# A PSUM bank for the convolution and tanh of a feed-forward, and another written order for its kernel

## The chip, the cores and the metric

The kernel runs on one core of a Trainium2 chip. The metric is the device time of one execution in microseconds (us). Three runs of the kernel before gave 747.68, 746.42 and 743.80 us, median 746.42. A separate execution was profiled; its own time was 744.24 us, and the span from its first to its last instruction 742.5 us.

Engines are called PE (matrix unit), DVE (vector), ACT (scalar, activations), POOL (GpSimd) and SP (issues the DMAs). Each runs its own instructions strictly in the order in which they were written for it, and waits on semaphores where it needs another engine's result.

## What is computed

```python
# q, k, v: (8, 8, 576, 64); window 128, ALiBi slopes per head
scores = q @ k.T / 8 + bias(slope, rel);  scores[not (0 <= rel < 128)] = -1e9
attn = softmax(scores);  x = (attn @ v) -> (batch, seq, 512)
h = relu(x @ w_in)                      # 512 -> 1024
conv_out[s] = sum_k conv_w[k] * h[s + k - 1]    # 3 taps along the sequence, zeros at its ends
out = (h * sigmoid(conv_out)) @ w_out   # 1024 -> 512
```

`w_in`, `conv_w` and `w_out` come in as 64-bit floats. The chip turns each into two single-precision parts, high and low, and every product with them is three matmuls: high by high, low by high, high by low.

## The kernel before

The 8 x 576 tokens are 36 tiles of 128. For each tile t and each half u of the heads (4 heads): `qkT` transposes q and k through PE, `scores` multiplies them against the keys of tiles t-1 and t, `merge` (DVE, L283 and L296) puts the window together in PSUM and adds the bias, `rowmax` (L300) and `exps` (ACT, L305) and `normal` (DVE, L316 to L318) make the softmax, `attnT` transposes it (L325, copied out by ACT, L328), two POOL masks (L331, L334) cut it into the sides of the window, and `av` multiplies by v. `x_hi` (ACT, L363) and `x_lo` (DVE, L367) split the result; `xfin` (L382, L384) copies one column of it to the neighbouring chunk. Some tiles lie at the joint of two sequences: tiles 4, 5, 13, 14, 22, 23, 31 and 32 need a second mask in each of their four merges, and tiles 0, 9, 18 and 27 begin a sequence and have only one side.

Two tiles make a chunk of 256 tokens for the feed-forward. A chunk has four steps, each for 256 of the 1024 hidden columns. A step is: `up_half` twice (24 matmuls, L406, then ACT's relu L410 to `hh` and the middle tap L411 to `z`), `conv` (DVE, L421: the outer two taps, for each of two halves, so four instructions, more at a joint), `gate` (ACT's tanh L429 in place, DVE L430), `split` (ACT L438, POOL L439) and `down` (12 matmuls, L454, into two PSUM banks that gather over the chunk's four steps). `hh` and `z` lie in SBUF, two buffers each. All other matmul results go through six PSUM banks that are handed out in turn (pool `pst`); `down` has two (`pso`).

A chunk's first step needs the column that `xfin` takes from the tile after the chunk: the matmuls of `up_half` wait for it in every second period.

What sets the order: within `manual_schedule` PE, DVE, ACT and POOL execute what the code calls in the order in which it calls it; SP's order was left to a planner. `opening()` (tiles 0 to 2), three slow periods (tiles 3, 4 and 5, which also convert the weights: `W`, 17 blocks of 128 x 512 or less), then `period(t)` for tiles 6 to 36 with two steps each, then `tail()` with the last four steps. A weight block is clamped by POOL (L130), rescaled by ACT (L131), put together by DVE (L137, L138, L141), rounded to its high part by ACT (L186), and PE (L201, L202) and ACT (L203) make the low part.

Of the kernel before, what the change touches and what calls it, by code (L numbers as in the profile page):

```python
# [8 lines left out]
F32 = mybir.dt.float32  # L9
# [7 lines left out]
P = 128  # L17
# [4 lines left out]
def tile_alibi_window_attention_conv_glu(  # L22
# [28 lines left out]
    pst = ctx.enter_context(tc.tile_pool(name="pst", bufs=6, space=bass.MemoryType.PSUM))  # L51
# [105 lines left out]
    fetched, begun, started = [], [], []  # L157

    def fetch_weight():
        if not blocks:  # L160
            return
        block = blocks.pop(0)
        st = wpool.tile([P, WB, 2], U32, name="wst", tag="wst")
        if block is None:
            n = 3 * NFC
            st = st[:n, :P, :]
            src = moe_conv_w.rearrange("k (f p) -> (k f) p", p=P).bitcast(U32).rearrange("r (p t) -> r p t", t=2)
        else:
# [12 lines left out]

    def convert_weight():
        block, st, g = begun.pop(0)
        f = to_f32(st, g)
        if block is not None:
            nc.scalar.copy(out=block[1][0], in_=f)  # L186
        started.append((block, f))
        fetch_weight()


    def finish_weight():
        block, f = started.pop(0)
        if block is None:
            n = 3 * NFC
            ps = pst.tile([P, n], F32, name="pcw", tag="tr")
            nc.tensor.transpose(ps, f, ident[:n, :n])
            nc.vector.tensor_copy(out=cw.rearrange("p k f -> p (k f)"), in_=ps)
# [14 lines left out]
    raws, vraw, pts, sms, es, rls, avs = {}, {}, {}, {}, {}, {}, {}  # L212
# [45 lines left out]
    def scores(t, u):  # L258
        first, slot, win, prev, cur = window(t)
        e = apool.tile([P, HU, P], F32, name=f"e{t}_{u}", tag="e", bufs=4)  # L260
        st = apool.tile([P, 3, HU], F32, name=f"st{t}_{u}", tag="st", bufs=3)
# [59 lines left out]
    def attnT(t, u):  # L321
# [15 lines left out]
        rls[t, u] = rl  # L337
# [374 lines left out]
```

## Time and profile before

| | us |
|---|---|
| median of three runs | 746.42 |
| time of the profiled execution | 744.24 |
| its span | 742.5 |
| PE busy | 663.2 (89%) |
| DVE busy | 559.9 (75%) |
| ACT busy | 451.7 (61%) |
| POOL busy | 205.0 (28%) |
| longest in the chain that ended last | DVE 52%, ACT 30%, PE 14% |

Busy times are sums over instructions; they say nothing of where an engine stood still. For that one cuts the span into stretches, here three: until the scores of tile 6 begin (150.7 us), until those of tile 35 begin (676.4 us), and the rest. A wait in the profile names the engine whose semaphore came last.

### The profile page before, as it was taken

The numbers are of one execution on the slowest core, as the hardware profiler recorded it, in microseconds if no ns is written. First come the engines' busy times: TensorE is split into PE (matmuls) and PEld (weight loads), VectorE is DVE, ScalarE is ACT, GpSimd is POOL, SyncE is SP. The second block draws the span as 40 slices with busy tenths as digits, with TensorE's granted clock in tenths as the row PEclk, the third lists the DMA queues.
The fourth block names the chain that finished last, engine by engine and source line by source line (L and its number), as shares of the span: only waits on it lengthen the run. The fifth ranks groups of instructions, "written<-read, shape, count | busy, mean of one in ns | idle before, by whom it ended". The sixth has DMA issues, their size and how long they took to land.

```text
span 742.5 us, 13277 instructions
## 1 busy us (share of the span) xinstructions
PE 663.2 (89%) x4881; PEld 565.6 (76%) x4881; DVE 559.9 (75%) x1208; ACT 451.7 (61%) x1274; POOL 205.0 (28%) x234
## 2 busy tenths in 40 slices
PE   6585868699989998999898999899899989998997
PEld 4354546588878887888787888788787878887896
DVE  7767665668887888888887878878888788888552
ACT  4656463566666666666666665666666656566653
POOL 1232222223223223322323333332223223322221
PEclk8878789899999999999999999999999999999999
DMA  9443331121222121212231232222221212100001
GB/s 221 107 128 94 119 87 43 28 73 44 72 57 57 44 72 43 72 44 72 44 86 55 46 86 44 61 55 72 57 59 44 72 43 72 43 29 1 30 1 57
DMA packets 120100, 47.02 MB, mean 63 GB/s; under 512 B 113356, under 2 KB 113380, under 8 KB 120036
## 3 DMA queue, kind: packets, MB, share of 16 engines
q1 hardware_dynamic: 120036, 46.17, 24.6%
q8 instruction: 39, 0.64, 0.4%
q14 instruction: 25, 0.20, 0.1%
HBM read 36.72 MB, written 9.44 MB: 62 GB/s over the span
## 4 chain that ended last, share of the span: by engine, by line
DVE 52%; ACT 30%; PE 14%; issue 3%; POOL 1%; DMA 1%; ACTq 0%; SPq 0%; DVEq 0%; POOLq 0%
DVE z L421 19%; ACT e L305 11%; DVE sc L283 6%; DVE st L300 6%; DVE e L296 6%; PE p L406 5%; ACT z L429 5%; DVE z L430 5%; ACT z L411 4%; PE o L454 4%; DVE x L367 3%; ACT hh L410 2%; ACT x L363 2%; ACT qkT_all L247 2%; DVE e L318 2%
## 5 line engine op out<-in xcount | busy, mean ns | idle before, releaser
L406 PE MATMUL p<-x,wi 128*128 128x258 f32 x1728 | 230.3, 291 | 28.7 <-DVE x L382 28.6
L406 PEld LDWEIGHTS p<-x,wi 128*128 128x128 f32 x1728 | 220.7, 195 | 36.9 <-ACT e L305 31.9
L421 DVE SCALAR_TENSOR_TENSOR z<-hh,cw,z 128x256 f32<-128x256 f32 (+7 forms) x384 | 196.3, 554 | 28.0 <-ACT z L411 24.5
L305 ACT ACTIVATE e<-e,st 128x128 f32<-128x128 f32 x288 | 112.7, 393 | 132.5 <-DVE st L300 132.1
L454 PE MATMUL o<-wo,gh 128*128 128x512 f32 x576 | 187.7, 407 | 2.3 <-ACT wo L203 1.9
L439 POOL TENSOR_TENSOR gl<-z,gh 128x512 fp32r<-128x512 f32 x72 | 94.3, 1309 | 146.7 <-ACT gh L438 142.8
L331 POOL TENSOR_SCALAR_AFFINE_SELECT rl<-rl 128x512 f32<-128x512 f32 x64 | 43.4, 678 | 329.5 <-ACT rl L328 329.2
L454 PEld LDWEIGHTS o<-wo,gh 128*128 128x128 f32 x576 | 103.3, 189 | 28.3 <-issue 4.5
L454 PE MATMUL o<-wo,gl 128*128 128x512 f32 x288 | 114.4, 397 | 0.0
L430 DVE SCALAR_TENSOR_TENSOR z<-z,hh 128x512 f32<-128x512 f32 x72 | 54.7, 760 | 61.5 <-ACT z L429 61.5
L429 ACT ACTIVATE z<-z 128x512 f32<-128x512 f32 x72 | 45.8, 636 | 72.5 <-DVE z L421 72.5
L411 ACT ACTIVATE z<-hh,cw 128x256 f32<-128x256 f32 x144 | 73.5, 510 | 9.2 <-ACT hh L410 0.8
L271 PE MATMUL sc<-qkT_all 64*128 64x256 f32 x512 | 68.8, 409 | 2.6 <-ACT qkT_all L247 2.6
L352 PE MATMUL av<-rl,rv 128*64 128x128 f32 x1088 | 68.7, 278 | 0.7 <-POOL rl L334 0.6
L352 PEld LDWEIGHTS av<-rl,rv 128*64 128x64 f32 x1088 | 59.4, 138 | 12.8 <-issue 7.7
L334 POOL TENSOR_SCALAR_AFFINE_SELECT rl<-rl 128x512 f32<-128x512 f32 x72 | 54.6, 758 | 41.8 <-ACT rl L328 37.4
L271 PEld LDWEIGHTS sc<-qkT_all 64*128 64x128 f32 x512 | 49.3, 197 | 21.0 <-issue 6.1
L296 DVE SCALAR_TENSOR_TENSOR e<-sc,bias 128x256 f32<-128x256 f32 x144 | 61.1, 425 | 4.9
L283 DVE COPY_PREDICATED sc<-m_prev,sc 128x256 f32<-128x256 uint8 x128 | 53.9, 421 | 14.1 <-PE sc L271 14.1
L454 PEld LDWEIGHTS o<-wo,gl 128*128 128x128 f32 x288 | 54.4, 189 | 13.2 <-POOL gl L439 0.2
L410 ACT ACTIVATE hh<-p 128x258 f32<-128x258 f32 x144 | 53.9, 374 | 6.7 <-PE p L406 6.5
L438 ACT CAST gh<-z 128x512 fp32r<-128x512 f32 x72 | 44.5, 618 | 20.1 <-DVE z L430 20.1
(64 smaller groups left out, 651.3 us busy)
## 6 DMA issues: line engine op xcount, KB each, us to landing
out_dram<-ob SPq DMA_DIRECT2D x36, 256.0 KB, 2.2
rqk<-in_q_dram SPq DMA_DIRECT2D x32, 256.0 KB, 3.3
rqk<-in_k_dram SPq DMA_DIRECT2D x32, 256.0 KB, 3.8
rv<-in_v_dram SPq DMA_DIRECT2D x32, 256.0 KB, 3.0
wst<-in_moe_w_in_dram SPq DMA_DIRECT2D x8, 512.0 KB, 4.8
wst<-in_moe_w_out_dram SPq DMA_DIRECT2D x8, 512.0 KB, 3.7
rqk<-in_q_dram SPq DMA_DIRECT2D x8, 128.0 KB, 3.2
rqk<-in_k_dram SPq DMA_DIRECT2D x8, 128.0 KB, 3.2
```

The lines of the kernel that those rows point to most:

```text
L271: nc.tensor.matmul(pss[a][:, g], qt, qkT_all[rows, win, u, 1, g, :], start=True, stop=True)
L283: nc.vector.copy_predicated(out=s_cur, mask=mask.unsqueeze(1).to_broadcast(shp), data=data)
L296: nc.vector.scalar_tensor_tensor(out=heads, in0=s_cur, scalar=-0.125, in1=b, op0=ALU.mult, op1=ALU.add)
L305: nc.scalar.activation(out=e[:, j, :], in_=e[:, j, :], func=AF.Exp, bias=st[:, 0, j : j + 1], scale=-1.0, accum_out=st[:, 1, j : j + 1],)
L352: nc.tensor.matmul(ps[a * D : (a + 1) * D, u * NG + g], vraw[tt][:, u * HU + j], rl[:, side, j], start=n == 0, stop=n == len(sides) - 1,)
L406: nc.tensor.matmul(ps[:, :XW], a[:, cc, f * P : (f + 1) * P], x[:, cc, :], start=n == 0, stop=n == last)
L411: nc.scalar.activation(out=z[:, ff, :], in_=hh[:, ff, 1 : 1 + CW], func=AF.Copy, scale=cw[:, 1, f : f + 1])
L421: nc.vector.scalar_tensor_tensor(out=z[:, ff, a:cut], in0=hh[:, ff, a + kk : cut + kk], scalar=cw[:, kk, f : f + 1], in1=z[:, ff, a:cut], ...
L429: nc.scalar.activation(out=z, in_=z, func=AF.Tanh)
L430: nc.vector.scalar_tensor_tensor(out=z, in0=z, scalar=1.0, in1=hh[:, :, 1 : 1 + CW], op0=ALU.add, op1=ALU.mult)
L439: nc.gpsimd.tensor_tensor(out=gl, in0=z, in1=as32(gh), op=ALU.subtract)
L454: nc.tensor.matmul(oo[m], g[:, ff, ms], w[:, f, :], start=f == 0 and n == 0, stop=f == NFC - 1 and n == 2)
```

## The change

The feed-forward's `z` is now two things. The middle tap, the convolution and the tanh work in place in `zp`, a tile of one PSUM bank with a single buffer (pool `psz`); `gate` reads `zp` and `hh` and writes `z` in SBUF, from which `split` goes on. The bank comes from `pst`, which has five in place of six.

Helpers are cut into smaller pieces (`relu`, `middle`, `conv`, `tanh`, `gate`, `g_hi`, `g_lo`, `down`, `store`; a weight block's six pieces; `attnT` without its copy and masks; `x_lo` without `xfin`), and the order of all of them is written in two strings: OPENING (tiles 0 to 5, steps 0 to 5, all weights) and PERIOD, used from tile 6 on until all is done. In a string, `MA0.1.0` is `merge(t+0, 1, 0)`, `XL-1` is `x_lo(t-1)`, `CV1.0` is `conv(s+1, 0)`, and `V3` is weight block 3's DVE part. SP's order is the written one too. The copy of `cw` out of PSUM moves from DVE to ACT.

```diff
-    pst = ctx.enter_context(tc.tile_pool(name="pst", bufs=6, space=bass.MemoryType.PSUM))
+    pst = ctx.enter_context(tc.tile_pool(name="pst", bufs=5, space=bass.MemoryType.PSUM))
+    psz = ctx.enter_context(tc.tile_pool(name="psz", bufs=1, space=bass.MemoryType.PSUM))
...
-            nc.scalar.activation(out=z[:, ff, :], in_=hh[:, ff, 1 : 1 + CW], func=AF.Copy, scale=cw[:, 1, f : f + 1])
+    def middle(s, ff):
+        f = 2 * (s % NFP) + ff
+        if s not in zps:
+            zps[s] = psz.tile([P, 2, CW], F32, name=f"zp{s}", tag="zp")
+        nc.scalar.activation(
+            out=zps[s][:, ff, :], in_=hhs[s][:, ff, 1 : 1 + CW], func=AF.Copy, scale=cw[:, 1, f : f + 1]
+        )
...
+    def conv(s, ff):
+        c, f = s // NFP, 2 * (s % NFP) + ff
+        hh, z = hhs[s], zps[s]
...
+    def tanh(s):
+        nc.scalar.activation(out=zps[s], in_=zps[s], func=AF.Tanh)
+
+    def gate(s):
+        zgs[s] = fpool.tile([P, 2, CW], F32, name=f"z{s}", tag="z", bufs=2)
+        nc.vector.scalar_tensor_tensor(
+            out=zgs[s], in0=zps.pop(s), scalar=1.0, in1=hhs.pop(s)[:, :, 1 : 1 + CW], op0=ALU.add, op1=ALU.mult
+        )
...
+    OPENING = """
+    Q0 QO0 CL0 S0.0 Q1 MA0.0.0 RS0 MA0.0.1 V0 S0.1 MA0.1.0 RM0.0 MA0.1.1 QO1 CL1 Q2 H0 P0 CL2 QO2 RS1 V1
...
+    PERIOD = """
+    S0.0 S0.1 MA0.0.0 AV-1 MA0.0.1 D-2 OB-2 XH-1 XL-1 GH-1 RM0.0 X0.0.1 XF-1 MA0.1.0 UH0.0 MA0.1.1
+    X0.0.0 RM0.1 N0.0 UH0.1 GL-1 Q1 HH0.0 Z0.0 CV0.0 UH1.0 X0.1.0 HH0.1 Z0.1 X0.1.1 CV0.1 QO1 UH1.1 N0.1
+    T0.0 TH0 HH1.0 GT0 RL0.0 T0.1 HH1.1 SEL0.0 Z1.0 CV1.0 Z1.1 CV1.1 RL0.1 GH0 TH1 SEL0.1 D-1 OB-1 GT1
+    GL0
+    """
...
-    with tc.manual_schedule(engines={engines.PE, engines.DVE, engines.Activation, engines.Pool}):
-        opening()
-        period(3, (2, 2, 2), first=False)
...
+    with tc.manual_schedule(engines={engines.PE, engines.DVE, engines.Activation, engines.Pool, engines.SP}):
...
+        emit(OPENING)
+        for t in range(FIRST, NT + 4):
+            emit(PERIOD, t, 2 * (t - FIRST) + 6)
```

Three places show what moved. First PE in the opening, before: tile 2's transposes (pa), tile 3's q and k (pt), then three weight blocks (pw) and behind them tile 3's scores (sc).

```order
L325 MATMUL pa_1_413<-ident_r,e_1_349 128x128 x4
L243 MATMUL pt_0_422<-ident_r,rqk_195 128x128 x4
L243 MATMUL pt_1_427<-ident_r,rqk_195 128x128 x4
L201 MATMUL pw<-wg,ident_r 128x512
L202 MATMUL pw<-wi_113,nident 128x512
L201 MATMUL pw<-wg,ident_r 128x512
L202 MATMUL pw<-wi_113,nident 128x512
L201 MATMUL pw<-wg,ident_r 128x512
L202 MATMUL pw<-wi_113,nident 128x512
L271 MATMUL sc_0_0_477<-qkT_all 128x256
```

The same engine and place now, around tile 3's scores.

```order
L236 MATMUL pt_1_491<-ident_r,rqk_177 128x128 x4
L320 MATMUL pa_1_517<-ident_r,e_1_404 128x128 x4
L320 MATMUL pa_0_523<-ident_r,e_0_373 128x128 x4
L191 MATMUL pw_528<-wg_419,ident_r 128x512
L192 MATMUL pw_528<-wi_116,nident 128x512
L262 MATMUL sc_0_0_538<-qkT_all 128x256
L262 MATMUL sc_0_1_539<-qkT_all 128x256
L262 MATMUL sc_0_0_538<-qkT_all 128x256
L262 MATMUL sc_0_1_539<-qkT_all 128x256
L191 MATMUL pw_552<-wg_421,ident_r 128x512
L192 MATMUL pw_552<-wi_116,nident 128x512
```

The weight blocks, which stood three in a row ahead of the scores, stand one at a time between pieces of the attention.

Second DVE in period 24, before: the merges of tile 24 (sc24, e24), tile 23's `x_lo` (L367) and `xfin` (L384; L382 where tile t-1 is a chunk's first).

```order
L283 COPY_PREDICATED sc24_0_1_5016<-m_prev_88,sc24_0_1_5016 128x2x128
L296 SCALAR_TENSOR_TENSOR e24_0_5013<-sc24_0_1_5016,bias_104 128x2x128
L300 TENSOR_REDUCE st24_0_5014<-e24_0_5013 128x4
L283 COPY_PREDICATED sc24_1_0_5023<-m_prev_88,sc24_1_0_5023 128x2x128
L296 SCALAR_TENSOR_TENSOR e24_1_5021<-sc24_1_0_5023,bias_104 128x2x128
L367 TENSOR_TENSOR x11_4639<-av23_5034,x11_4639 128x4x128
L384 CAST x12_5059<-x11_4639 128x8
```

The same stretch of DVE now (with the new file's line numbers, here and in the other two places), with the last convolution and gate of period 23 ahead of it.

```order
L422 SCALAR_TENSOR_TENSOR zp41_5020<-hh41_5006,cw_120,zp41_5020 128x256 x4
L433 SCALAR_TENSOR_TENSOR z41_5053<-zp41_5020,hh41_5006 128x512
L278 COPY_PREDICATED sc24_0_0_5056<-m_prev_91,sc24_0_0_5056 128x2x128
L291 SCALAR_TENSOR_TENSOR e24_0_5068<-sc24_0_0_5056,bias_107 128x2x128
L278 COPY_PREDICATED sc24_0_1_5057<-m_prev_91,sc24_0_1_5057 128x2x128
L291 SCALAR_TENSOR_TENSOR e24_0_5068<-sc24_0_1_5057,bias_107 128x2x128
L366 TENSOR_TENSOR x11_4690<-av23_5072,x11_4690 128x4x128
L295 TENSOR_REDUCE st24_0_5069<-e24_0_5068 128x4
L382 CAST x12_5115<-x11_4690 128x8
```

`x_lo` stands ahead of the row maximum and of the third merge, `xfin` ahead of the third merge.

Third ACT in period 24, before, with what each row waits for: relu, middle tap and tanh of step 42 (z10_2, its number within chunk 10).

```order
L410 ACTIVATE hh10_2_5087<-p10_4_5089 128x258 [waits PE_49]
L411 ACTIVATE z10_2_5088<-hh10_2_5087,cw_117 128x256 [waits Activation_49,Pool_49]
L410 ACTIVATE hh10_2_5087<-p10_5_5104 128x258 [waits PE_49]
L411 ACTIVATE z10_2_5088<-hh10_2_5087,cw_117 128x256 [waits Activation_49]
L247 COPY qkT_all_118<-pt25_0_5122 128x512 [waits PE_49]
L247 COPY qkT_all_118<-pt25_1_5127 128x512 [waits PE_49]
```

The same step on ACT now.

```order
L403 ACTIVATE hh42_5169<-p42_0_5121 128x258 [waits PE_49]
L409 ACTIVATE zp42_5171<-hh42_5169,cw_120 128x256 [waits Activation_49]
L300 ACTIVATE e24_1_5117,st24_1_5118<-e24_1_5117,st24_1_5118 128x128 [waits DVE_49]
L300 ACTIVATE e24_1_5117,st24_1_5118<-e24_1_5117,st24_1_5118 128x128
L403 ACTIVATE hh42_5169<-p42_1_5142 128x258 [waits PE_49]
L409 ACTIVATE zp42_5171<-hh42_5169,cw_120 128x256 [waits DVE_49,Activation_49]
L300 ACTIVATE e24_1_5117,st24_1_5118<-e24_1_5117,st24_1_5118 128x128 x2
L240 COPY qkT_all_124<-pt25_0_5156 128x512 [waits PE_49]
L240 COPY qkT_all_124<-pt25_1_5161 128x512 [waits PE_49]
L429 ACTIVATE zp42_5171<-zp42_5171 128x512 [waits DVE_49]
```

The second half's middle tap waits for DVE, which it did not, and two exponentials and the two copies of q and k stand behind it.

## Rows read from the trace of the kernel before

**Rows 1.** The page's first and second part: PE's busy time, share and instructions; the granted clock in 40 slices, in tenths of full speed.

```profile
PE 663.2 (89%) x4881; PEld 565.6 (76%) x4881; DVE 559.9 (75%) x1208; ACT 451.7 (61%) x1274; POOL 205.0 (28%) x234
...
PEclk8878789899999999999999999999999999999999
```

**Rows 2.** Busy time by stretch (until tile 6's scores, until tile 35's, the rest): length, then PE, weight loads, DVE, ACT, POOL with instructions, granted clock, DMA share and GB/s.

```profile
0.00:150.70 150.70, 103.83 (x585) 75.26 (x585) 99.86 (x216) 81.37 (x213) 36.38 (x53) 0.82 0.40 104
150.70:676.40 525.70, 500.56 (x3897) 439.14 (x3896) 424.12 (x928) 337.27 (x984) 151.83 (x166) 0.99 0.23 57
676.40:742.50 66.10, 58.82 (x401) 51.15 (x400) 35.89 (x65) 33.08 (x78) 16.81 (x16) 1.00 0.07 25
```

**Rows 3.** Who waited for whom, PE in the middle stretch: us in total, times, longest.

```profile
PE p L406 <- DVE x L382: 24.4, 12, 3.2
PE pa L325 <- DVE e L318: 0.7, 1, 0.7
```

**Rows 4.** Busy time by stretch, as rows 2: first two single periods, then the score matmuls alone (L271, and L269 for a sequence's first tile; 16 a tile) in the middle stretch.

```profile
168.46:185.65 17.19, 17.19 (x137) 15.20 (x137) 13.56 (x35) 11.35 (x33) 4.47 (x5) 1.00 0.21 47
...
601.39:623.50 22.11, 18.92 (x137) 16.61 (x137) 18.27 (x36) 12.23 (x35) 7.97 (x9) 0.92 0.17 37
...
150.70:676.40 525.70, 52.49 (x416) 38.43 (x416) 0.99 0.23 57
...
150.70:676.40 525.70, 3.49 (x48) 2.91 (x48) 0.99 0.23 57
```

**Rows 5.** The timeline of a period with a long stall of PE: start, us, instruction, and idle time before it with what ended it.

```profile
601.39 2.00 PE L271 MATMUL sc<-qkT_all 64*128 64x256 f32 x16
...
601.77 2.43 DVE L421 SCALAR_TENSOR_TENSOR z<-hh,cw,z 128x128 f32<-128x128 f32 x4 [0.47 <-ACT z L411]
...
602.39 0.70 POOL L331 TENSOR_SCALAR_AFFINE_SELECT rl<-rl 128x512 f32<-128x512 f32 x1
...
604.29 0.63 ACT L429 ACTIVATE z<-z 128x512 f32<-128x512 f32 x1 [2.08 <-DVE z L421]
604.96 0.69 DVE L430 SCALAR_TENSOR_TENSOR z<-z,hh 128x512 f32<-128x512 f32 x1 [0.75 <-ACT z L429]
...
605.57 0.42 DVE L283 COPY_PREDICATED sc<-m_prev,sc 128x256 f32<-128x256 uint8 x1
...
606.02 0.49 DVE L283 COPY_PREDICATED_SCALAR sc<-m_half,neg 128x256 f32 x1
...
606.39 1.30 POOL L439 TENSOR_TENSOR gl<-z,gh 128x512 fp32r<-128x512 f32 x1 [2.59 <-ACT gh L438]
...
606.54 0.42 DVE L296 SCALAR_TENSOR_TENSOR e<-sc,bias 128x256 f32<-128x256 f32 x1
...
609.83 0.56 ACT L363 CAST x<-av 128x512 fp32r<-128x512 f32 x1
...
610.42 0.69 DVE L367 TENSOR_TENSOR x<-av,x 128x512 fp32r<-128x512 f32 x1
...
611.15 0.17 DVE L382 CAST x<-x 128x8 fp32r<-128x8 f32 x1
...
611.47 4.51 PE L406 MATMUL p<-x,wi 128*128 128x258 f32 x24 [3.19 <-DVE x L382]
...
613.27 0.16 DVE L316 TENSOR_SCALAR st<-st 128x4 f32<-128x4 f32 x1
...
613.68 0.69 DVE L318 TENSOR_TENSOR e<-e,st 128x512 f32<-128x512 f32 x1
...
616.10 1.92 DVE L421 SCALAR_TENSOR_TENSOR z<-hh,cw,z 128x256 f32<-128x256 f32 x4
...
617.19 3.15 PE L406 MATMUL p<-x,wi 128*128 128x258 f32 x24
```

**Rows 6.** Groups of instructions by line and shape: count, busy us, mean ns of one, idle before.

```profile
L421 DVE SCALAR_TENSOR_TENSOR z<-hh,cw,z 128x256 f32<-128x256 f32 x176 | 115.0, 670 | 23.3 <-ACT z L411 20.1
L305 ACT ACTIVATE e<-e,st 128x128 f32<-128x128 f32 x288 | 112.7, 393 | 132.5 <-DVE st L300 132.1 <-DVE st L316 0.4
...
L411 ACT ACTIVATE z<-hh,cw 128x256 f32<-128x256 f32 x144 | 73.5, 510 | 9.2 <-ACT hh L410 0.8
...
L296 DVE SCALAR_TENSOR_TENSOR e<-sc,bias 128x256 f32<-128x256 f32 x144 | 61.1, 425 | 4.9
...
L410 ACT ACTIVATE hh<-p 128x258 f32<-128x258 f32 x144 | 53.9, 374 | 6.7 <-PE p L406 6.5
L283 DVE COPY_PREDICATED sc<-m_prev,sc 128x256 f32<-128x256 uint8 x128 | 53.9, 421 | 14.1 <-PE sc L271 14.1
...
L300 DVE TENSOR_REDUCE st<-e 128x4 f32<-128x512 f32 x72 | 49.4, 686 | 2.5
...
L438 ACT CAST gh<-z 128x512 fp32r<-128x512 f32 x72 | 44.5, 618 | 20.1 <-DVE z L430 20.1
...
L247 ACT COPY qkT_all<-pt 128x512 f32<-128x512 f32 x72 | 38.2, 579 | 4.7 <-PE pt L243 4.7
```

**Rows 7.** PE's longest wait in the first stretch (as rows 3), and the timeline's first work of PE and first merge of DVE.

```profile
PE pw L201 <- DVE wg L141: 25.4, 6, 6.7
...
4.34 0.66 PE L243 MATMUL pt<-ident_r,rqk 128*128 128x128 f32 x2 [4.34 <-DMA rqk<-in_q_dram]
...
7.93 0.49 DVE L283 COPY_PREDICATED_SCALAR sc<-m_prev,neg 128x256 f32 x1 [3.32 <-PE sc L269]
```

More of the change, by code (lines that the diff above doesn't have):

```diff
@@ L182, in convert_weight @@
[L182 to L197, printed above, removed]
+        wst[b] = st
@@ L336, in attnT @@
         )
-        rls[t, u] = rl
     def av(t):
@@ L549, in opening, with up @@
-    def opening():
+    NFP = NFC // 2
+    hhs, zps, zgs, gs, oos = {}, {}, {}, {}, {}
+    def up(s, ff):
+        c, f = s // NFP, 2 * (s % NFP) + ff
+        hi, lo = xch[c][:, 0], xch[c][:, 1]
+        ps = pts[s, ff, "up"] = pst.tile([P, 512], F32, name=f"p{s}_{ff}", tag="tr")
+        n, last = 0, 3 * NCC - 1
+        for cc in range(NCC):
+            for a, x in ((wi[0], hi), (wi[0], lo), (wi[1], hi)):
+                nc.tensor.matmul(
+                    ps[:, :XW], a[:, cc, f * P : (f + 1) * P], x[:, cc, :], start=n == 0, stop=n == last
+                )
+                n += 1
@@ new lines, in g_lo, with down @@
+    def g_lo(s):
+        gh, gl = gs[s]
+        nc.gpsimd.tensor_tensor(out=gl, in0=zgs.pop(s), in1=as32(gh), op=ALU.subtract)
+    def down(s):
+        c, fp = divmod(s, NFP)
+        if c not in oos:
+            oos[c] = [pso.tile([P, DM], F32, name=f"o{c}_{m}", tag="o") for m in range(CT)]
+        gh, gl = gs.pop(s)
+        order = [(ff, m) for ff in range(2) for m in range(CT)]
+        if fp == NFP - 1:
+            order = [(ff, m) for m in range(CT) for ff in range(2)]
+        for ff, m in order:
+            f = 2 * fp + ff
+            ms = slice(m * P, (m + 1) * P)
+            for n, (g, w) in enumerate(((gh, wo[0]), (gh, wo[1]), (gl, wo[0]))):
+                nc.tensor.matmul(
+                    oos[c][m], g[:, ff, ms], w[:, f, :], start=f == 0 and n == 0, stop=f == NFC - 1 and n == 2
+                )
@@ new lines, in store @@
+    def store(s):
+        c, fp = divmod(s, NFP)
+        if fp < NFP - 1:
+            return
+        for m, o in enumerate(oos.pop(c)):
+            ob = fpool.tile([P, DM], F32, name=f"ob{c}_{m}", tag="ob", bufs=2)
+            nc.scalar.copy(out=ob, in_=o)
+            g0 = c * CW + m * P
+            nc.sync.dma_start(out=out_flat[g0 : g0 + P, :], in_=ob)
+        xch.pop(c)
+    def qk(t):
+        for u in range(2):
+            qkT(t, u)
+        if t + 2 < NT:
+            load(t + 2)
@@ new lines, in qk_out, with attn_v @@
+    def qk_out(t):
+        for u in range(2):
+            qkT_out(t, u)
+    def attn_v(t):
+        av(t)
+        if t + 3 < NT:
+            loadv(t + 3)
+    TILE = {
+        "Q": qk, "QO": qk_out, "S": scores, "MA": merge, "RM": rowmax,
+        "X": lambda t, u, h: exps(t, u, range(2 * h, 2 * h + 2)),
+        "N": normal, "T": attnT, "RL": attn_out, "SEL": select, "AV": attn_v, "XH": x_hi, "XL": x_lo, "XF": xfin,
+    }
+    STEP = {
+        "UH": up, "HH": relu, "Z": middle, "CV": conv, "TH": tanh, "GT": gate, "GH": g_hi, "GL": g_lo,
+        "D": down, "OB": store,
+    }
```

403 lines of the change are left out of this document (108 added, 295 removed).

## The prediction, as put on record

> **What bounds the kernel now.** I read the busy times and the clock first, then the span cut into three stretches, then PE's waits in each, then one period of the timeline with the longest wait in it.
>
> PE is busy 663.2 of 742.5 us [rows 1], but not evenly. [...] So there are three prices: 46.9 us without PE in the opening, 25.1 in the middle, 7.3 at the end. DVE, whose share of the ending chain is the largest, is busy for no more than 81% of the middle stretch; it matters by when it delivers, not by its sum.
>
> In the middle stretch PE's idle time has one cause: 24.4 us in 12 waits of the first-layer matmuls L406 for `xfin` L382; the next is 0.7 [rows 3]. These are odd periods, where a chunk begins. A period without the wait takes 17.19 us with PE busy throughout; the one at 601.39 takes 22.11 [rows 4]. The stretch holds 416 + 48 score matmuls, 16 a tile, so 29 periods [rows 4].
>
> The timeline of that period shows how the wait is made [rows 5]. DVE's convolution (601.77) takes 2.43 us while POOL masks (602.39), the tanh comes at 604.29, the gate at 604.96, and only at 605.57 does DVE begin the merges, though their matmuls began at 601.39. `x_lo` follows three merges and a row maximum later (610.42), `xfin` at 611.15, and PE, which had waited 3.19 us, starts at 611.47 and runs those 24 matmuls in 4.51 us; the next 24, at 617.19, take 3.15. The clock had fallen (0.92 over the period), so a long wait costs some 1.4 us more than itself.
>
> **The convolution.** Four instructions of 256 columns take 1.92 us at 616.10, 0.48 each [rows 5], but 0.670 on average [rows 6]. L296, of the same size, takes 0.42 at 606.54 with POOL at work [rows 5], and 0.425 on average [rows 6]; it has one input from PSUM, while L421 has both from SBUF. With `z` in PSUM the convolution has L296's placement. The trace doesn't show this form with PSUM as output and a per-partition factor. Its bounds: 0.42 (L296) and 0.67 (L421 as now); I take 0.48, as now beside no POOL work. Over 8 a period that is 8 x 0.19 = 1.5 us of DVE. The gate gets one PSUM input too and I take its 0.69 [rows 5]. The middle tap stays between 0.37 (L410) and 0.51 (L411) [rows 6]; I take 0.45.
>
> The row of L367, with an input from PSUM, shows 0.69, as does the gate at 604.96 with both inputs from SBUF [rows 5]. [...]
>
> **The bank.** Both halves of a step lie in one bank, and ACT's second middle tap now waits for DVE (the order of ACT shows it), that is for the first half's convolution; behind it stand two exponentials and the copies of q and k. No row of before has such a wait, so its price comes from a walk through a period. [...] By addresses alone the second tap would come a microsecond earlier in the walk, and the total would be about 6 us less (690); the written waits are by bank, and so is the sum.
>
> **A period's walk.** Zero is the start of the scores, PE's next scores come at 17.2. Five banks hold: each is wanted again five allocations later, and in this walk its reader is through a microsecond or more before that. I start DVE's merges at 3.0 (found by going round twice). Each merge is 0.42 + 0.42 [rows 6], 0.9 with gaps: two end at 4.8. `av` ends at 3.8, `x_hi` 0.56 [rows 5] at 4.5; `x_lo` 0.69 to 5.5, row maximum 0.69 [rows 6] to 6.2, `xfin` at 6.4. PE has 12 `down` matmuls between `av` and the first layer and wants it at 6.6. It is there: in an ordinary period the wait goes. Two merges and a row maximum later DVE is at 8.9. Normalising is 1.05 (613.27 to the end at 614.37 [rows 5]), to 10.0; first half's convolution to 11.0; ACT's second tap to 11.5; second half's to 12.5; second normalising to 13.6. ACT has two exponentials of 0.39, two copies of 0.58 (L247 [rows 6]) and the tanh of 0.63 behind its tap and is through at 14.1, the gate at 14.8. ACT then does relu 0.37 (L410), a copy as long as L247's, another relu and the tap, to 16.0; convolution 17.0, tap 17.5, convolution 18.5; a copy, the cast 0.62 (L438 [rows 6]) and the tanh stand on ACT to 19.5; the gate ends at 20.2, which is 3.0 of the next period. It closes, PE staying the bound, with 0.2 us to spare at `xfin` and about 1 at the masks ahead of `av`.
>
> In six periods (tiles 13, 14, 22, 23, 31, 32) each merge has a second mask of 0.49 (606.02 [rows 5]): the merges then end 2 us later, the second normalising comes at about 15.5, and PE wants it for its transposes at 14.05: a stall of 1.5. Six of them cost 9 us, between 0 (PE catches up) and 15 (the odd ones wait at `xfin` too).
>
> Middle stretch: 525.7 - 24.4 (waits) - 3 x 1.4 (the clock behind the three longest) + 9 = 506. Bounds: 495 (29 periods at 17.19, less 3 us for shorter tiles) and 526 (nothing gained).
>
> **The opening.** PE's longest wait there is for weights: 25.4 us in 6 waits of L201 for DVE's L141 [rows 7]. Three blocks stood in a row ahead of the scores; now they stand singly, each many DVE instructions behind its own conversion. All steps, tiles and weights are as many as before, so the floors are what the engines work: PE 103.83 + 4.34 until its first matmul, DVE 99.86 + 7.93 until its first merge [rows 2, 7], both about 108. The ceiling is 150.7. What share of the stretch will the busier engine fill? Now it is 103.83/150.7 = 0.69; in the middle stretch 0.95 [rows 2]. The opening stays harder than the middle, since PE, DVE and ACT (81.4) are nearly level and each waits for the others, but the waits named are mostly for order. I take 0.85: 103.83/0.85 = 122, 28.7 us less. DMAs issue in the written order, and the queue waits in turn for a buffer's reader; the mean load in the opening is 0.40 [rows 2], so I count nothing, and up to 10 us if the second and third weight blocks arrive late.
>
> **The end.** The last steps run at PE's pace before and now. The single bank makes the last steps follow each other more strictly: 0 to 3 us more, against up to 3 less. I keep 66.1.
>
> **Sum.** 122 + 506 + 66 = 694 of span; the profiled execution's time is 1.74 us above its span, so 696 where it took 744.24. The median of runs lay 2.2 higher, 0.3%, which I leave inside the range. Predicted: 696 us.
>
> **Rivals.**
> 1. Both stretches reach their floors: 110 + 497 + 66 + 2 = 675. For it: every wait named is for order alone. Against it: three engines level in the opening.
> 2. The opening is held by something the order can't mend, weights that land late or the slow clock: 140 + 510 + 66 + 2 = 718. For it: clock 0.82 where PE stands often. Against: DMA 0.40 busy.
> 3. Slower: the bank's loop becomes the bound of every period. If the convolution goes on being held up by POOL, as its `hh` still comes from SBUF, and every one of the eight took twice its 0.48 (the 0.67 of rows 6 is a mean of held and free ones), 8 x 0.48 = 3.8 us are added to a loop with no more than 1 us to spare: a period of 20, 29 x 20 + 122 + 66 + 2 = 770. It decides from (742.5 - 122 - 66)/29 = 19.1 us a period. Against it: L296 at 606.54 also reads one operand from SBUF and isn't held up.
> 4. The change doesn't do what it says: the waits for `xfin` stay because DVE begins its merges no earlier, and the opening's gain is lost in the same way: within 0.5% of before.
>
> **How the numbers follow.** Forecast 0.55 (682 to 712), rival 1 0.20, rival 2 0.17, rival 3 0.05, rival 4 0.03. The range takes in the forecast, most of rival 1 and half of rival 2: 668 to 724. About 0.5% (3.7 us) is what a measurement of this kernel can tell from no change. Faster 0.92, same 0.03, slower 0.05.
>
> **What would show it.** The convolution's group at 0.48 with no long tail; the wait of the first layer for `xfin` gone or under 8 us in all; ordinary periods at 17.2 and the six with second masks at 18.5 to 19; the scores of tile 6 at about 122 us, with the wait of L201's successor for weights gone; the second tap's wait for DVE visible on ACT, without PE waiting behind it. Wrong: a period above 18 everywhere (the bank), or tile 6 after 135 us (the opening).

## The result and the profile after

Three runs of the changed kernel took 696.86, 696.92 and 697.87 us, median 696.92, where 696 was predicted; its time is 0.9346 of the kernel before (95% interval 0.9305 to 0.9388). The profiled execution took 697.87 us, its span is 696.1. The total came out within a microsecond, in part because errors cancel: the runs below show that the new written order earns all of the gain, and that the bank takes a part of it back.

The page after, first and second part, as [rows 1]:

```profile
PE 654.1 (94%) x4881; PEld 555.6 (80%) x4881; DVE 521.1 (75%) x1207; ACT 444.1 (64%) x1275; POOL 191.5 (28%) x234
...
PEclk9989999999999999999999999999999999999999
```

Busy time by stretch, as [rows 2] (until tile 6's scores, until tile 35's, the rest):

```profile
0.00:119.50 119.50, 96.34 (x585) 69.57 (x585) 92.74 (x212) 77.32 (x211) 31.68 (x51) 0.96 0.50 128
119.50:625.40 505.90, 496.19 (x3897) 434.04 (x3896) 397.04 (x933) 334.11 (x987) 143.24 (x168) 1.00 0.24 59
625.40:696.10 70.70, 61.58 (x401) 51.95 (x400) 31.30 (x64) 32.65 (x78) 16.55 (x16) 0.98 0.06 23
```

The opening is 31.2 us shorter, the middle 19.8, the end 4.6 longer. Who waited for whom, as [rows 3]: first PE's longest wait of the middle, then the longest of ACT and of DVE there, then PE's of the end.

```profile
PE pa L320 <- DVE e L313: 9.7, 18, 0.6
...
ACT zp L409 <- DVE zp L422: 61.6, 58, 1.7
...
DVE zp L422 <- ACT zp L409: 56.6, 87, 1.0
...
PE o L459 <- ACT ob L469: 2.3, 1, 2.3
PE o L459 <- ACT gh L440: 1.3, 2, 0.7
PE o L459 <- POOL gl L445: 1.2, 2, 0.6
```

The first layer's wait for `xfin` (24.4 us in [rows 3]) is gone from the middle. In its place PE waits 18 times for some half a microsecond, for the second normalising of a tile. The second middle tap and the convolution now wait for each other. Where that leads is seen in single periods, as [rows 4]: two that follow each other, a third (tile 13's), and the convolution alone in stretches that hold the two steps of the first two.

```profile
119.65:136.78 17.13, 17.13 (x138) 15.12 (x137) 13.08 (x30) 11.79 (x35) 4.78 (x6) 1.00 0.31 78
136.78:154.65 17.87, 17.38 (x137) 15.13 (x137) 13.88 (x35) 10.95 (x34) 5.08 (x6) 1.00 0.21 45
240.97:259.15 18.18, 17.61 (x137) 15.07 (x136) 14.56 (x35) 11.09 (x34) 5.08 (x6) 1.00 0.20 44
...
121.15:138.28 17.13, 3.91 (x8) 1.00 0.31 78
138.28:156.15 17.87, 5.68 (x16) 1.00 0.21 45
```

The second period holds 16 convolution instructions where the first holds 8: a sequence begins inside its chunk, and each of the taps is cut there. Twelve of the 29 periods are of this kind (17.85 to 17.89 us each), six others (tiles 13, 14, 22, 23, 31, 32) have the second masks (17.87 to 18.18); each of them holds one of the 18 waits (12 with 6.3 us in all, 6 with 3.4), and no other period has one. The timeline of the second one:

```profile
136.78 2.00 PE L262 MATMUL sc<-qkT_all 64*128 64x256 f32 x16
...
141.35 0.69 DVE L366 TENSOR_TENSOR x<-av,x 128x512 fp32r<-128x512 f32 x1 [0.78 <-ACT x L362]
...
142.55 0.68 DVE L380 CAST x<-x 128x8 fp32r<-128x8 f32 x1
...
143.51 3.06 PE L395 MATMUL p<-x,wi 128*128 128x258 f32 x24
...
146.47 1.52 DVE L422 SCALAR_TENSOR_TENSOR zp<-hh,cw,zp 128x64 f32<-128x64 f32 x4
...
148.08 0.48 ACT L409 ACTIVATE zp<-hh,cw 128x256 f32<-128x256 f32 x1 [0.96 <-DVE zp L422]
148.59 1.53 DVE L422 SCALAR_TENSOR_TENSOR zp<-hh,cw,zp 128x64 f32<-128x64 f32 x4 [0.61 <-ACT zp L409]
...
150.44 0.69 DVE L313 TENSOR_TENSOR e<-e,st 128x512 f32<-128x512 f32 x1
...
151.28 0.30 PE L320 MATMUL pa<-ident_r,e 128*128 128x128 f32 x1 [0.49 <-DVE e L313]
```

First half's convolution, second tap, second half's convolution stand in a chain on two engines, the second normalising behind it, and PE's transposes wait for that. The groups by line and shape, as [rows 6]:

```profile
L422 DVE SCALAR_TENSOR_TENSOR zp<-hh,cw,zp 128x256 f32<-128x256 f32 x176 | 86.0, 489 | 58.5 <-ACT zp L409 55.3
L409 ACT ACTIVATE zp<-hh,cw 128x256 f32<-128x256 f32 x144 | 69.1, 480 | 70.6 <-DVE zp L422 67.5 <-DVE z L433 1.9
L433 DVE SCALAR_TENSOR_TENSOR z<-zp,hh 128x512 f32<-128x512 f32 x72 | 49.7, 690 | 34.1 <-ACT zp L429 34.1
...
L382 DVE CAST x<-x 128x8 fp32r<-128x8 f32 x17 | 10.1, 592 | 0.0
```

And what is left in the opening, as [rows 7]: PE's longest wait there is now for tile 2's load, DVE's for the second weight block's rescaling; PE's wait for weights is down from 25.4 us to 0.7.

```profile
PE pt L236 <- DMA rqk<-in_q_dram: 10.9, 3, 5.8
...
PE pw L191 <- DVE wg L174: 0.7, 1, 0.7
...
DVE wg L171 <- ACT wg L164: 6.9, 1, 6.9
```

### The profile page after: what moved, and what is told of

Its sections match the earlier page's. It is cut to its first block, busy times and chain, and to the rows that moved or that the text cites. A ratio compares the mean times of both kernels' runs of the same rounds, so it can differ in the third digit from the quotient of the medians.

```text
span 696.1 us, 13391 instructions
## 1 busy us (share of the span) xinstructions
PE 654.1 (94%) x4881; PEld 555.6 (80%) x4881; DVE 521.1 (75%) x1207; ACT 444.1 (64%) x1275; POOL 191.5 (28%) x234
## 4 chain that ended last, share of the span: by engine, by line
PE 52%; DVE 34%; ACT 8%; issue 3%; DMA 2%; SPq 1%; POOL 1%; ACTq 0%; DVEq 0%; POOLq 0%
PE o L459 18%; PE p L395 13%; DVE zp L422 10%; PE sc L262 7%; PE av L351 7%; DVE sc L278 5%; DVE st L295 4%; DVE e L313 4%; DVE e L291 4%; PE pa L320 3%; ACT zp L409 3%; PE pt L236 2%; DVE x L366 2%; DMA rqk<-in_k_dram 2%; PE pw L191 1%
## 5 line engine op out<-in xcount | busy, mean ns | idle before, releaser
L422 DVE SCALAR_TENSOR_TENSOR zp<-hh,cw,zp 128x256 f32<-128x256 f32 (+7 forms) x384 | 162.0, 422 | 89.8 <-ACT zp L409 81.3
L395 PE MATMUL p<-x,wi 128*128 128x258 f32 x1728 | 224.0, 286 | 2.8 <-DVE x L380 2.8
L395 PEld LDWEIGHTS p<-x,wi 128*128 128x128 f32 x1728 | 215.6, 191 | 8.8 <-issue 5.3
L445 POOL TENSOR_TENSOR gl<-z,gh 128x512 fp32r<-128x512 f32 x72 | 92.5, 1285 | 114.4 <-ACT gh L440 100.7
L331 POOL TENSOR_SCALAR_AFFINE_SELECT rl<-rl 128x512 f32<-128x512 f32 x64 | 40.6, 635 | 289.2 <-ACT rl L325 289.2
L409 ACT ACTIVATE zp<-hh,cw 128x256 f32<-128x256 f32 x144 | 69.1, 480 | 70.6 <-DVE zp L422 67.5
L433 DVE SCALAR_TENSOR_TENSOR z<-zp,hh 128x512 f32<-128x512 f32 x72 | 49.7, 690 | 34.1 <-ACT zp L429 34.1
L320 PE MATMUL pa<-ident_r,e 128*128 128x128 f32 x288 | 42.5, 277 | 16.4 <-DVE e L313 12.1
L362 ACT CAST x<-av 128x512 fp32r<-128x512 f32 x36 | 21.3, 591 | 56.5 <-PE av L351 56.5
L334 POOL TENSOR_SCALAR_AFFINE_SELECT rl<-rl 128x512 f32<-128x512 f32 x72 | 45.9, 638 | 39.7 <-ACT rl L325 28.8
```

What stands on the lines that cost most here:

```text
L320: nc.tensor.transpose(ps[:, j, :], e[:, j, :], ident)
L395: nc.tensor.matmul(ps[:, :XW], a[:, cc, f * P : (f + 1) * P], x[:, cc, :], start=n == 0, stop=n == last)
L409: nc.scalar.activation(out=zps[s][:, ff, :], in_=hhs[s][:, ff, 1 : 1 + CW], func=AF.Copy, scale=cw[:, 1, f : f + 1])
L422: nc.vector.scalar_tensor_tensor(out=z[:, ff, a:cut], in0=hh[:, ff, a + kk : cut + kk], scalar=cw[:, kk, f : f + 1], in1=z[:, ff, a:cut], ...
L445: nc.gpsimd.tensor_tensor(out=gl, in0=zgs.pop(s), in1=as32(gh), op=ALU.subtract)
```

## The experiments

Times are medians; a ratio is to the kernel before on the same chip, with its 95% interval. "Middle" is the stretch from tile 6's scores to tile 35's, in one profiled execution of each run. Runs e1 to e4 were measured on one chip, e5 to e8 on a second and e9 to e12 on a third, so totals of different groups are compared by their ratios.

**e1: z back in SBUF, the new order kept.**

```diff
-    psz = ctx.enter_context(tc.tile_pool(name="psz", bufs=1, space=bass.MemoryType.PSUM))
...
-            zps[s] = psz.tile([P, 2, CW], F32, name=f"zp{s}", tag="zp")
+            zps[s] = fpool.tile([P, 2, CW], F32, name=f"zp{s}", tag="zp", bufs=1)
```

> The changed kernel with its new order, five banks for the rest as there, but z of the convolution back in SBUF (one buffer). Placement theory: the convolution instructions that lie beside POOL's masks and its subtraction take about 0.96 us again where the changed kernel has 0.49, their mean rises from 0.49 to 0.60-0.70, a period with masks beside the second step gets 0.5 to 1.5 us longer, and the total is 705 to 740 us. Rival, order alone: the order has moved the convolution out of POOL's way, the mean stays under 0.55 and the total within 0.5% of 697; it may even be under that, since the second middle tap no longer waits for the first half's convolution by bank.

Measured: 691.76 us, ratio 0.9265 (0.9227 to 0.9303). Middle, PE's wait there and the convolution's group:

```profile
120.30:619.40 499.10, 493.97 (x3897) 434.34 (x3896) 417.63 (x932) 333.72 (x988) 156.65 (x170) 1.00 0.25 60
...
PE p L394 <- DVE x L379: 5.1, 5, 1.3
...
L421 DVE SCALAR_TENSOR_TENSOR zp<-hh,cw,zp 128x256 f32<-128x256 f32 x176 | 105.6, 612 | 41.5 <-ACT zp L408 38.0
```

Each theory is half right. The convolution is slower again (612 ns against 489), as the placement theory said. Its mechanism is read from the trace of the kernel before: there 72 of the 176 whole pieces lie beside work of POOL and take 0.94 us on average, the other 104 take 0.48. But the kernel is faster, not slower, and below the rival's 0.5%, for the reason that the rival had allowed for. The middle is 6.8 us shorter than with the bank: PE is the bound, DVE's extra 20 us lie beside it, and the wait for the second normalising is gone with the bank.

**e2: the bank alone, in the kernel before with its old order.**

```diff
-    pst = ctx.enter_context(tc.tile_pool(name="pst", bufs=6, space=bass.MemoryType.PSUM))
+    pst = ctx.enter_context(tc.tile_pool(name="pst", bufs=5, space=bass.MemoryType.PSUM))
+    psz = ctx.enter_context(tc.tile_pool(name="psz", bufs=1, space=bass.MemoryType.PSUM))
...
-            z = fpool.tile([P, 2, CW], F32, name=f"z{c}_{fp}", tag="z", bufs=2)
+            z = psz.tile([P, 2, CW], F32, name=f"zp{c}_{fp}", tag="zp")
...
+            g = fpool.tile([P, 2, CW], F32, name=f"z{c}_{fp}", tag="z", bufs=2)
             nc.vector.scalar_tensor_tensor(
-                out=z, in0=z, scalar=1.0, in1=hh[:, :, 1 : 1 + CW], op0=ALU.add, op1=ALU.mult
+                out=g, in0=z, scalar=1.0, in1=hh[:, :, 1 : 1 + CW], op0=ALU.add, op1=ALU.mult
             )
+            gs[fp] = hh, g
```

> The kernel before with its old order, only z of the convolution in one PSUM bank (five banks for the rest). Placement theory: the convolution falls from 0.67 to 0.48 us, DVE begins the merges 1 us or more earlier after the second step, the 24.4 us in which the first layer waits for xfin shrink to 5 to 12, and the total is 725 to 735 us. Rival: one bank where two SBUF buffers stood ties a step to the gate of the step before, this takes back what the convolution gives, and the total stays within 0.5% of 746.

Measured: 799.45 us, ratio 1.0699 (1.0662 to 1.0737). Both theories miss: the bank, with the single buffer and the loss of the sixth bank that come with it, makes the kernel 7% slower. The middle is 571.0 us (525.7 in [rows 2]), and the wait for `xfin` has grown:

```profile
PE p L407 <- DVE x L383: 35.1, 14, 4.4
```

**e3: the old opening, everything else as changed.** OPENING, the string of the opening, is replaced by one with the same pieces in the order in which the kernel before wrote them.

> The changed kernel's period and tail with the opening in the old written order (same pieces, z in PSUM). Theory of independent parts: the scores of tile 6 begin at 145 to 151 us instead of 119.6, the middle stays at 506, and the total is 723 to 730 us. Rival, the opening's gain comes from something that the new period brings with it or from the faster convolution: tile 6 by 135 us and a total under 714.

Measured: 728.78 us, ratio 0.9754 (0.9720 to 0.9788). The theory of independent parts holds: tile 6 begins at 149.6 us, the middle is 506.1.

```profile
0.00:149.70 149.70, 103.65 (x587) 74.78 (x587) 95.75 (x215) 81.26 (x214) 33.57 (x53) 0.86 0.39 102
149.70:655.80 506.10, 496.14 (x3897) 434.08 (x3896) 395.17 (x929) 332.67 (x984) 140.94 (x165) 1.00 0.24 59
```

**e4: the old period, opening and bank as changed.**

```diff
-    S0.0 S0.1 MA0.0.0 AV-1 MA0.0.1 D-2 OB-2 XH-1 XL-1 GH-1 RM0.0 X0.0.1 XF-1 MA0.1.0 UH0.0 MA0.1.1
...
+    GH-1 GL-1 S0.0 S0.1 MA0.0.0 MA0.0.1 RM0.0 AV-1 X0.0.0 MA0.1.0 XH-1 XL-1 XF-1 X0.0.1 MA0.1.1 RM0.1 D-2 OB-2
+    N0.0 X0.1.0 X0.1.1 UH0.0 HH0.0 Z0.0 UH0.1 HH0.1 Z0.1 N0.1 Q1 QO1 CV0.0 CV0.1 T0.0 RL0.0 SEL0.0 TH0 GT0
+    UH1.0 HH1.0 Z1.0 GH0 GL0 UH1.1 HH1.1 Z1.1 CV1.0 CV1.1 T0.1 RL0.1 SEL0.1 TH1 GT1 D-1 OB-1
```

> The changed kernel's opening with the period in the old written order (z in PSUM). Theory of independent parts: tile 6 at 119 to 122 us, and the middle between 506 and 526 by as much as the placement gives: with placement 510 to 518, so a total of 698 to 710 us. Rival, the new order of the period makes the whole gain of the middle: 522 to 528 there, 711 to 718 in all, with the first layer waiting 20 us or more for xfin.

Measured: 774.90 us, ratio 1.0355 (1.0317 to 1.0392). Both theories miss here too: the middle is 570.9 us, as in e2. So the price of the bank depends on the order: 45 us in the old one, with the single buffer and the lost sixth bank in it. e7 and e8 take that apart.

**e7 and e8: the old period with z in SBUF, one buffer and two.** As e4, with the allocation of e1, `bufs=1` in e7 and `bufs=2` in e8.

> The changed kernel's opening, the period in the old order, z in SBUF but with a single buffer, five banks for the rest. Single-buffer theory: what made the old order slow with the bank (middle 571 us where it had 525.7) is that a step's middle tap must wait for the gate of the step before; then the middle is 565 us or more here too and the total 765 to 785. Rival, the bank itself (its waits by bank, or the reads of PSUM): the middle is 520 to 535 here and the total 712 to 728.

> As the run before it, but with two buffers of z in SBUF, as the old order was made for; five banks for the rest. Single-buffer theory: the middle is back at 522 to 530 us and the total 713 to 722, that is the new opening's gain alone. Rival, five banks in place of six are the cause: the middle stays at 545 or more and the total at 740 or more.

Measured: e7 744.61 us, ratio 0.9992 (0.9971 to 1.0013); e8 720.91 us, ratio 0.9670 (0.9623 to 0.9717). The middle of e8, then of e7, then of e4:

```profile
123.10:653.30 530.20, 507.35 (x3897) 442.58 (x3896) 424.41 (x931) 341.57 (x988) 155.82 (x168) 0.98 0.23 57
...
122.40:670.90 548.50, 512.17 (x3897) 445.17 (x3896) 428.67 (x932) 337.86 (x987) 157.28 (x169) 0.98 0.23 55
...
122.10:693.00 570.90, 515.84 (x3897) 447.00 (x3896) 396.09 (x928) 336.33 (x984) 144.02 (x168) 0.97 0.22 53
```

e8's total comes out as expected and its middle 0.2 us above the range, which leaves some 4.5 us at most (530.2 against 525.7, and e8's profiled execution was the slowest of its four) for the loss of the sixth bank. In e7 neither theory is enough: a single buffer costs 18.3 us, the bank another 22.4. The second figure is the one to set beside e1's 6.8, which also compares bank and SBUF with one buffer and five other banks. e3 and e8 answer one more rival: the change also gave SP a written order, moved the copy of `cw` and gave the tile `st` five buffers in place of three, and with all of that the old opening still takes 149.6 us and the old period 530.2. The timelines show both. First e7, where z is in SBUF, then e4, where it is in the bank:

```profile
248.84 0.95 DVE L432 SCALAR_TENSOR_TENSOR z<-zp,hh 128x512 f32<-128x512 f32 x1 [0.83 <-ACT zp L428]
...
249.88 0.51 ACT L408 ACTIVATE zp<-hh,cw 128x256 f32<-128x256 f32 x1 [0.88 <-DVE z L432]
...
250.42 4.02 DVE L421 SCALAR_TENSOR_TENSOR zp<-hh,cw,zp 128x128 f32<-128x128 f32 x8 [0.64 <-ACT zp L408]
...
251.22 0.51 ACT L408 ACTIVATE zp<-hh,cw 128x256 f32<-128x256 f32 x1
```

```profile
234.98 0.69 DVE L433 SCALAR_TENSOR_TENSOR z<-zp,hh 128x512 f32<-128x512 f32 x1 [0.79 <-ACT zp L429]
...
235.77 0.48 ACT L409 ACTIVATE zp<-hh,cw 128x256 f32<-128x256 f32 x1 [0.60 <-DVE z L433]
...
237.10 0.48 ACT L409 ACTIVATE zp<-hh,cw 128x256 f32<-128x256 f32 x1
...
237.61 3.09 DVE L422 SCALAR_TENSOR_TENSOR zp<-hh,cw,zp 128x128 f32<-128x128 f32 x8 [1.94 <-ACT zp L409]
```

In both, the step's first tap waits for the gate of the step before: that is the single buffer. In SBUF the convolution starts as the first tap ends and runs beside the second. In the bank it starts only behind the second tap, 1.84 us after the first began where SBUF has 0.54. The old order writes both taps ahead of the convolution, and so pays this in nearly every step (in e4 between 200 and 500 us, some 15 periods of two steps, the convolution waits 31 times for a tap, 41.8 us in all; over the whole run the idle time of DVE that a tap ends ahead of the whole pieces is 71.3 us in e4 and 31.2 in e7); the new one writes the first half's convolution between the taps.

**e5: the second normalising ahead of the second half's convolution, z in the bank.**

```diff
-    X0.0.0 RM0.1 N0.0 UH0.1 GL-1 Q1 HH0.0 Z0.0 CV0.0 UH1.0 X0.1.0 HH0.1 Z0.1 X0.1.1 CV0.1 QO1 UH1.1 N0.1
...
+    X0.0.0 RM0.1 N0.0 UH0.1 GL-1 Q1 HH0.0 Z0.0 CV0.0 UH1.0 X0.1.0 X0.1.1 HH0.1 Z0.1 N0.1 CV0.1 QO1
...
```

> The changed kernel (z in the bank) with the second normalising written ahead of the second half's convolution, and the second pair of exponentials of the second half ahead of the relu before it. Theory of the bank wait: PE's wait for the second normalising goes (9.7 us in 18 waits), ordinary periods fall from 17.9 to 17.2, the middle to 497 to 501 us as with z in SBUF, and the total to 689 to 693. Rival, the single bank's loop of tap, convolution, tanh and gate is itself as long as a period: the wait moves to the masks or to the first layer, periods stay at 17.7 or more and the total within 0.5% of 697.

Measured: 690.11 us, ratio 0.9252 (0.9220 to 0.9285). The theory of the bank wait holds: PE's wait for the second normalising is gone, and what is left is a little for `xfin` and the masks.

```profile
119.50:617.10 497.60, 494.02 (x3897) 434.09 (x3896) 390.63 (x931) 335.32 (x985) 143.11 (x168) 1.00 0.25 60
...
PE p L395 <- DVE x L380: 2.1, 2, 1.0
```

**e6: each half of z in a bank of its own, four banks for the rest.**

```diff
-    pst = ctx.enter_context(tc.tile_pool(name="pst", bufs=5, space=bass.MemoryType.PSUM))
+    pst = ctx.enter_context(tc.tile_pool(name="pst", bufs=4, space=bass.MemoryType.PSUM))
...
-            zps[s] = psz.tile([P, 2, CW], F32, name=f"zp{s}", tag="zp")
+            zps[s] = psz.tile([P, 2, 512], F32, name=f"zp{s}", tag="zp")[:, :, :CW]
```

> The changed kernel with each half of z in a bank of its own (two banks for z, four for the rest), order as it is. If the wait within the bank alone costs the 6.8 us that the middle has above the one with z in SBUF, the second tap no longer waits for the first half's convolution, the middle is 497 to 501 us and the total 689 to 694. Rival: four banks are too few, PE waits for a bank's reader ahead of the first layer or the transposes, and the total is 700 or more.

Measured: 763.80 us, ratio 1.0249 (1.0202 to 1.0295). The rival holds: PE waits ahead of `av` for the merges that free a bank. And the kernel did not test what it was meant to: the second tap still waits for the first half's convolution, though their banks now differ. Why the program keeps that wait is not shown (the halves are one tile here, but so they are in e7, where in SBUF the second tap does not wait). Whether two banks without it would help stays open.

```profile
PE av L351 <- DVE e L291: 42.5, 25, 2.8
...
ACT zp L409 <- DVE zp L422: 51.4, 49, 1.7
```

**e9 to e12: the changed kernel again, and two more edits on e5.** e10 gives the steps behind the last tile an order of their own; e11 edits the opening; e12 has both.

```diff
...
+    TAIL = """
+    UH0.0 HH0.0 Z0.0 CV0.0 UH0.1 HH0.1 Z0.1 CV0.1 D-2 OB-2 TH0 GT0 GH0 GL0 UH1.0 HH1.0 Z1.0 CV1.0
+    UH1.1 HH1.1 Z1.1 CV1.1 D-1 OB-1 TH1 GT1 GH1 GL1
+    """
...
-        loadv(1)
-        loadv(2)
...
-    Q0 QO0 CL0 S0.0 Q1 MA0.0.0 RS0 MA0.0.1 V0 S0.1 MA0.1.0 RM0.0 MA0.1.1 QO1 CL1 Q2 H0 P0 CL2 QO2 RS1 V1
+    Q0 QO0 CL0 S0.0 Q1 MA0.0.0 RS0 MA0.0.1 V0 LV1 LV2 S0.1 MA0.1.0 RM0.0 MA0.1.1 QO1 CL1 Q2 H0 P0 CL2 RS1 QO2 V1
```

> The changed kernel once more, beside the versions built on it, so that differences of half a per cent can be read on one chip: 697 us within 0.3%.

> The version with the second normalising first (690 us), and with an order of its own for the last steps, which have no attention: each second-layer piece two steps behind its first layer and between two first-layer halves. Theory of the tail: PE's 4.8 us of waits for the cast, the subtraction and the output copies after tile 35 shrink to 1 or 2, and the total falls by 3 to 4 us to 686 or 687. Rival: the last chain of tap, convolution, tanh, gate and subtraction ends the kernel in either order, and the total stays within 0.2% of 690.

> The version with the second normalising first, and two edits of the opening: the second weight block's rescaling on ACT ahead of the copies of tile 2's q and k, and the loads of v for tiles 1 and 2 written behind the fourth weight block's. Theory of the opening's waits: DVE's 6.9 us wait for that rescaling and PE's 5.8 us for tile 2's load shrink by 3 us or more, and tile 6 begins 2 to 5 us earlier, total 685 to 688. Rival: the opening is held further on by conversions of weights, and tile 6 begins within 1 us of 119.6.

> The three edits together. If they are independent: the sum of the gains of the two runs before this one, 681 to 685 us; if the opening's edits give nothing, 686 to 687.

Measured: e9 697.23 us, as expected (ratio 0.9350, 0.9325 to 0.9375), e10 685.70 (0.9194, 0.9170 to 0.9219), e11 687.78 (0.9219, 0.9193 to 0.9244), e12 683.54 (0.9174, 0.9150 to 0.9198). The end of e10 and the opening of e11:

```profile
618.90:684.60 65.70, 59.30 (x401) 50.93 (x400) 31.24 (x66) 33.27 (x79) 16.66 (x16) 1.00 0.07 25
```

```profile
0.00:117.00 117.00, 95.04 (x585) 69.45 (x585) 92.91 (x212) 77.23 (x211) 33.02 (x51) 0.96 0.50 131
...
DVE wg L171 <- ACT wg L164: 3.2, 2, 2.8
```

The tail theory holds: the end falls from 71.5 us in e5 to 65.7, the waits named from 4.8 to 1.5, and the total by 4.4, a little more than expected. The opening's edits halve DVE's wait, but PE's longest wait for a load falls only from 5.9 us in e5 to 4.2; e11 is 2.3 us below e5 and e12 2.2 below e10, but the intervals overlap, since the opening itself varies: 119.5 us in e5 and 121.3 in e10 without the edits, 117.0 in e11 and 119.4 in e12 with them. So this gain is likely, not shown. e12 is 6.6 us below e5, about the sum of both, and it beats both kernels: 2.0% under the changed one, measured beside it.

## Why the prediction was right, and where its steps were not

What was forecast did happen: the order shortens the opening by some 30 us, and PE no longer waits for `xfin`. That the total is met within a microsecond is luck: 2.5 us too much for the opening, 4.6 too little for the end, and a middle of 506 made up of terms that are wrong in opposite directions.

- **The opening: right in size.** 122 predicted, 119.5 measured, and e3 gives the old order's 149.6 back with nothing else moved. Two errors inside it cancel. PE's work in the stretch was taken as fixed at 103.83 us; it is 96.34, for the same 585 matmuls, at a granted clock of 0.96 where it was 0.82. And it fills 0.81 of the stretch, not 0.85. The 10 us held ready for late weights were not needed: DVE's 6.9 us wait is not for a late weight. The second block is there when POOL clamps it (12.16), but its rescaling (21.12) stands on ACT behind the copies of tile 2's q and k, whose load PE awaits until 18.01; e11, which writes it ahead of them, halves the wait.
- **The wait for `xfin`: gone, as predicted.** In the period shown `xfin` ends 6.45 us after the scores begin (predicted 6.4), and the first layer starts at 6.73 (predicted 6.6). The agreement has luck in it: the cast takes 0.68 us where the walk gave it 0.2, and the pieces ahead of it come earlier. But the walk left open whether the order or the convolution in PSUM does it, and the opening words of that part lean on the convolution. e1 shows that the order does most of it: with z in SBUF the wait is 5.1 us in 5 places.
- **The convolution: 0.48 a piece is right (0.489), its worth is not.** 1.5 us of DVE per period were counted. The line's busy time in the middle is 134.5 us (x328) where it was 159.8 (x324): 25.3 / 29 = 0.87 a period. The mean of 0.670 was too large a base: in the kernel before the records of two pieces can overlap (their durations add up to 175.9 us in that stretch), and most of the cut pieces gain less. On the path it is worth little. No run has e5's order with z in SBUF, so its worth is not isolated, but it is small: e5's middle is 1.5 us shorter than e1's, their totals cannot be told apart (ratios 0.9252 and 0.9265), and in e1, which lacks it, PE waits no more than 5.1 us in the whole middle.
- **The bank: total right, terms wrong.** By addresses 690 was worked out against 696 by bank; e1 took 691.8 and e5 690.1. But ordinary periods were put at 17.2 us "without PE waiting behind" the second tap, and the six with second masks at 1.5 us each. The step that failed is the walk's "first half's convolution to 11.0": it counts 1.0 us a half, and in 12 of the 29 periods a half is cut into four instructions and takes 1.52 [the timeline above]. [rows 5] had shown such a half: the line at 601.77 is 128x128, four of them. The second normalising then ends at 14.35, not 13.6, and PE wants it at 14.0. The six periods wait 0.55 to 0.57 us each and not 1.5, and last 17.87 to 18.18 us where 18.5 to 19 were foreseen. So two terms, 0 for the ordinary periods and 9 for the six, should have been 6.3 and 3.4 by the recorded waits: both wrong, their sum right. That the second tap's wait is by bank is the prediction's reading and not shown: e6 has two banks and keeps it (51.4 us in 49 places).
- **The waits cost more than their records.** By the lengths of the periods the two terms are larger: against the 17.13 us of the undisturbed period at 119.65, the twelve cost 8.8 us and the six 5.1, 13.9 together. The middle without them would be 492, not the walk's 525.7 - 24.4 - 4.2 = 497.1. So the old waits were priced too low by about as much as the new ones: 3 x 1.4 was added for the three longest alone, but the period from 238.25 to 256.79 of the kernel before, with a wait of 1.16 us, took 18.54. That e5 comes to 497.6 doesn't confirm the 497.1, since two of its periods wait for `xfin`.
- **The end: mis-sized.** 66.1 was kept, with up to 3 more; it is 70.7. Behind the last tile the second layer stands directly behind the cast and the subtraction that it reads, and behind the copies of its output (the 4.8 us of waits above). Of the 4.6 us more, 2.8 are PE's own work, 61.58 us in place of 58.82: behind the wait of 2.3 us the granted clock falls, from 1.00 to 0.74 between 671.8 and 674 and to 0.50 from 674 to 676. It is mostly the order and not the bank: with z in SBUF the end takes 69.5 us (e1), and e10's order gives 65.7. The two stretches behind that wait, as [rows 2]:

```profile
671.80:674.00 2.20, 2.20 (x7) 1.82 (x8) 0.24 (x1) 0.94 (x2) 1.18 (x1) 0.74 0.63 236
674.00:676.00 2.00, 2.00 (x6) 1.54 (x5) 0.00 (x0) 0.00 (x0) 0.09 (x1) 0.50 0.01 2
```

- **Rival 3 was given 0.05 and a wrong mechanism.** POOL does not hold the convolution with z in PSUM (of its 176 whole pieces 60 lie beside POOL's work, and none takes more than 0.49 us). But the bank does hold every step up where the order doesn't make room for it: e4 took 775 us where the rival said 770, by the single buffer and by the second tap ahead of the convolution. The forecast was safe only because the walk had been made with the new order.
- **The gate: 0.69 was taken, 0.690 measured.** With one operand from PSUM the 72 gates (L433) take 690 ns on average; with both from SBUF the gate took 0.69 in the kernel before [rows 5], and so on average did the 38 there that lie beside no work of POOL.

## What to carry to other kernels

Price a shared bank in the order that it will run in: here ACT's tap and DVE's convolution took turns in one bank (61.6 us of waits on one side, 56.6 on the other in the changed kernel's middle), a chain that cost 6.8 us in one written order and 22.4 in the other (45 with the single buffer and the lost sixth bank). A faster instruction on an engine that isn't the bound earned little here (in e1, which lacks it, PE waits only 5.1 us in the whole middle), so undo it alone before it is given the credit. A walk through a period must take each line's forms one by one: the mean of the commonest form hid the cut ones, which decided 12 of 29 periods. And a wait is to be priced by the length of the period that holds it: here its record was smaller than what it cost.

## What the hardware showed that was not expected

The casts of `xfin`, 8 elements a partition, take 592 ns on average (L382) where the kernel before had 175, and 0.68 in the timeline above. They now lie beside POOL's subtraction for `gl`, which reads two operands from SBUF: in the period at 535.90 it runs from 541.02 for 1.30 us and the cast from 541.66 for 0.69. In e4 the subtraction (242.97, 1.29 us) is over before the cast (246.64), and the cast takes 174 on average. Within the changed kernel alone the 34 casts split in the same way: the 8 that touch no subtraction take 0.16 to 0.18 us, and the 26 that begin during one take 0.51 to 0.69 and end 0.03 to 0.04 us behind it. No run moved that cast alone, so the cause is read from the traces and not shown by an experiment. The convolution, which now has one operand from SBUF and one from PSUM, keeps its 489 ns beside POOL (60 of its 176 whole pieces lie there, none over 0.49 us).

From e3 to the changed kernel only the order of the opening differs. PE stands idle 23 us there in place of 46, the mean granted clock rises from 0.86 to 0.96, and the same matmuls take 96.3 us in place of 103.7, which no step of the prediction had counted.
